# A later first branch hint and a finer last output block in a convolution and token-mixing kernel

## The chip, the cores and the metric

The kernel runs on one core of a Trainium2 chip. The metric is device time in microseconds (us) of one execution. It is some 1.9 us longer than the span that the profile shows. "Faster" or "slower" means by over 2%.

## The reference

The input x has 8 batches of 4224 tokens with 192 channels. A causal convolution of 7 taps, one softmaxed set of taps for each of 8 heads of 24 channels, is followed by a linear attention without softmax, a ReLU and an output product.

```python
def _attn_ref(x, weight):                    # weight: (8 heads, 7 taps)
    ...                                      # w = softmax(weight) over the taps
    out = np.einsum('hk,bskhg->bshg', w, x_unf)        # causal, 6 zeros ahead
    ...
def _moe_ref(x, w_q, w_k, w_out):
    wq = x @ w_q;  wk = x @ w_k
    W_tok = scale * np.einsum('bsd,btd->bst', wq, wk)
    mixed = np.einsum('bst,btd->bsd', W_tok, x)
    return np.maximum(mixed, 0.0) @ w_out
```

As nothing stands between the two products of the attention, the kernel forms the small matrix of each batch (a Gram matrix of the convolved y, with w_q and w_k around it) and multiplies the tokens by that.

## The kernel before

One program of some 5700 instructions is laid out ahead of time by a planner in the kernel's file. The names that the profile shows: xw is a staged piece of x, "ps<-xw,band" the convolution as a matmul with a band matrix, "ps<-y" the Gram matmuls, "ps<-yb,wq" the query product (Q), "ps<-qt,m_sb" the mixing (Z), "ps<-wo,zt" the output product (O), o_sb an output slot. Eight output slots of 768 KB serve in turn.

Two places are changed. The first is the class that puts branches and their hints into TensorE's stream, which it counts in blocks of 256 instructions: the page has 2456 matmuls, as many weight loads, and 19 instruction packets of 16 KB. A branch that goes to the next instruction anyway carries a hint, which is meant to have the next block fetched ahead; in the execution that the prediction read the first hint ran at 0.91 us and the first 16 KB fetch started at 2.01. Before, the first hint is TensorE's first action:

```python
class Ahead:
    HEAD, BLOCK, FROM = 64, 256, 128
    def __init__(self, nc, e):
        ...
        e.reg_mov(self.reg, 0)
        self.mark = e.mark_branch_hint_location()      # at 0.9 us
    def step(self, waits):
        if self.n >= self.cuts * self.BLOCK + self.FROM:
            self.cut()                                 # the branch, and the next hint
        ...
```

The second is the last full output block, which is cut into two jobs of two PSUM banks with one store each:

```python
            for j in range(2):
                cols = slice(2 * q + j, 512, 4)
                ...
            elif tail:
                parts = [(at + 2 * q * D, [[4 * D, 128], [HALF * D, 2], [1, 2 * D]],
                          OUT[:, orr, q, :].rearrange("p (h d) -> p h d", h=2))]
```

GpSimd issues nearly all loads of x, and between them it clears some tiles, in this order:

```python
    load(1, 3)
    load(2, 0)
    z_wo2 = pool(lambda e: e.memset(WO2[:, :], 0.0))
    load(2, 1)
```

WO2 is a zero-padded copy of a part of the output weights. The copies into it wait for this memset, and the planner's ORDER string puts the evictions of the first mixing matrix (m_sb) behind those copies.

## Time and profile before

| | before |
|---|---|
| time, first three timed runs | 154.13 to 154.24 us, median 154.21 |
| time, 46 further runs over five chips | 154.10 to 156.47 us |
| execution that the prediction read | 155.59 us, span 153.7 |
| a usual execution, profiled later | 154.22 us, span 152.3 |

The kernel has two kinds of execution: most take 154.1 to 155.0 us, and 14 of the 49 that were timed in all took 155.6 to 156.5. The page that the prediction read came from one of the second kind, while the time that it started from is of the first. The record lists the mean granted clock of nearly every run: it is 0.973 to 0.978 in all 19 long runs of the kernels that clear WO2 on GpSimd, and 0.984 or more in 70 of their 72 others. A stretch at half clock like the one on that page (0.50 from 11.75 to 15.16 us) takes 0.011 off the mean of a span of 153.7; so my estimate from these figures is that a long execution has one in it (and two usual ones too). Of the profiled executions that have one, those of r3 and r4 below are listed with 0.976 (155.92 us, long) and 0.975 (154.33 us, usual), that of the page with 0.982. In the prediction's lines a number pair such as "9.28 0.02" is a start and a duration in us, and in the windows there follow each engine's busy time and its instructions, the clock, the share of the DMA engines and GB/s.

### The profile page before, as it was taken

Reading aid. Unit: us, or ns where it says so; the run is one execution under the profiler, and the core shown is the slowest. Engines: PE = TensorE matmul, PEld = TensorE weight load, DVE = VectorE, ACT = ScalarE, POOL = GpSimd, SP = SyncE. Lnnn points to the kernel's source line nnn. Section 1 sums busy time; section 2 is a strip of 40 time slices with the busy share of each in tenths; the row PEclk is TensorE's granted clock in tenths of the full one; section 3 lists DMA queues with packets and bytes.
Section 4 is the critical chain, followed back from the end, with each engine's and each line's share of the span. In section 5 each row is a group of like instructions: output and inputs, shape, how many; then the busy total and the mean of one; then the engine's idle time right before and its main releaser. Section 6 shows DMA issues by size and latency. Waiting matters only on the chain.

```text
span 153.7 us, 5694 instructions
## 1 busy us (share of the span) xinstructions
PE 139.9 (91%) x2456; PEld 101.9 (66%) x2456; DVE 119.8 (78%) x239; ACT 128.2 (83%) x213; POOL 58.4 (38%) x76
## 2 busy tenths in 40 slices
PE   5647897999999999999999999999999999999930
PEld 1337774877777777677777777668677778775720
DVE  6544898988998878798989877999998988695800
ACT  5443869999998989989998989899899788999950
POOL 7999999997367620817200021120020200000000
PEclk9995999999999999999999999999999999999997
DMA  3999999999999999999999999999999967499795
GB/s 96 263 196 181 190 190 183 190 191 193 191 193 191 238 341 340 266 189 279 340 341 221 206 343 340 295 175 363 404 389 408 334 241 291 174 390 396 289 376 212
DMA packets 48440, 40.83 MB, mean 266 GB/s; under 512 B 37280, under 2 KB 40480, under 8 KB 48416
## 3 DMA queue, kind: packets, MB, share of 16 engines
q0 software_dynamic: 36384, 13.35, 73.4%
q1 hardware_dynamic: 12032, 27.14, 48.5%
q8 instruction: 19, 0.31, 0.7%
q14 instruction: 5, 0.04, 0.1%
HBM read 27.86 MB, written 25.95 MB: 350 GB/s over the span
## 4 chain that ended last, share of the span: by engine, by line
PE 78%; DVE 7%; DMA 5%; ACT 3%; issue 1%; SPq 1%; ACTq 0%
PE ps L194 78%; DMA o_sb<-in_x_dram 5%; DVE y L1021 2%; ACT y L1021 2%; DVE yb L1017 1%; DVE zt L1025 1%; DVE zr L1025 1%; DVE m_sb L1027 1%; DVE o_sb L1021 1%; ACT o_sb L1021 1%; DVE qt L1021 1%; DVE xw L1021 0%; ACT m_sb L1026 0%; ACTq L154 0%; ACT wo L1021 0%
## 5 line engine op out<-in xcount | busy, mean ns | idle before, releaser
L1021 ACT COPY o_sb<-ps 128x768 f32<-128x768 f32 (+1 forms) x61 | 47.3, 788 | 3.7 <-PE ps L194 2.6
L194 PE MATMUL ps<-wo,zt 128*128 128x192 bf16 (+1 forms) x358 | 47.5, 270 | 0.3 <-DVE o_sb L1021 0.2
L194 PEld LDWEIGHTS ps<-y 128*128 128x128 bf16 (+1 forms) x864 | 36.3, 99 | 12.5 <-issue 2.5
L1021 ACT CAST y<-ps 128x864 bf16<-128x864 f32 (+6 forms) x47 | 38.0, 834 | 7.5 <-PE ps L194 7.0
L194 PE MATMUL ps<-y 128*128 128x64 bf16 (+1 forms) x864 | 40.9, 195 | 1.2 <-DVE y L1021 1.2
L194 PEld LDWEIGHTS ps<-wo,zt 128*128 128x128 bf16 x358 | 31.9, 114 | 9.3 <-ACT zt L1024 0.7
L1017 DVE STREAM_TRANSPOSE yb<-y 128x576 int32<-128x576 int32 x48 | 35.7, 759 | 0.1
L194 PE MATMUL ps<-xw,band 128*128 128x432 bf16 (+5 forms) x192 | 32.3, 290 | 3.6 <-DVE xw L1021 2.0
L1021 POOL COPY y<-y 128x1152 bf16<-128x1152 bf16 x11 | 12.6, 1146 | 59.8 <-ACT y L1021 40.0
L1025 DVE TENSOR_SCALAR zt<-ps 128x512 bf16<-128x512 f32 x44 | 29.3, 679 | 4.8 <-PE ps L194 4.5
L326 POOL DMA_DIRECT2D xw<-in_x_dram x35 | 32.1, 928 | 2.0 <-POOL xw L485 1.1
L1024 ACT ACTIVATE zt<-ps 128x512 bf16<-128x512 f32 x52 | 30.3, 604 | 1.5 <-PE ps L194 1.4
L194 PE MATMUL ps<-qt,m_sb 128*128 128x512 bf16 (+2 forms) x120 | 30.8, 344 | 0.5 <-ACT m_sb L1026 0.5
L1021 DVE CAST y<-ps 128x864 bf16<-128x864 f32 (+2 forms) x21 | 21.5, 1024 | 3.6 <-PE ps L194 3.1
L194 PEld LDWEIGHTS ps<-xw,band 128*128 128x128 bf16 x192 | 13.8, 100 | 8.8 <-DVE xw L1021 2.3
L1021 DVE CAST qt<-ps 128x288 bf16<-128x288 f32 (+1 forms) x32 | 12.3, 425 | 7.2 <-PE ps L194 7.2
L194 PE MATMUL ps<-yb,wq 32*64 32x288 bf16 x768 | 15.2, 284 | 0.3 <-ACT y L1021 0.3
L1021 ACT CAST qt<-ps 128x576 bf16<-128x576 f32 x16 | 10.3, 643 | 3.4 <-PE ps L194 2.7
L194 PEld LDWEIGHTS ps<-qt,m_sb 128*128 128x128 bf16 (+1 forms) x120 | 8.9, 96 | 5.0 <-ACT m_sb L1026 0.8
L194 PEld LDWEIGHTS ps<-yb,wq 32*64 32x64 bf16 x768 | 10.5, 102 | 2.6 <-issue 0.7
L194 PE MATMUL ps<-warm 128*128 128x256 bf16 (+1 forms) x21 | 6.4, 420 | 1.3 <-DVE warm L377 1.3
L1021 DVE COPY o_sb<-ps 128x192 f32<-128x192 f32 (+1 forms) x11 | 6.8, 618 | 0.9 <-PE ps L194 0.6
(65 smaller groups left out, 72.8 us busy)
## 6 DMA issues: line engine op xcount, KB each, us to landing
out_dram<-o_sb SPq DMA_DIRECT2D x31, 768.0 KB, 7.2
xw<-in_x_dram POOLq DMA_DIRECT2D x14, 432.0 KB, 15.9
xw<-in_x_dram POOLq DMA_DIRECT2D x14, 384.0 KB, 16.9
o_sb<-in_x_dram SPq DMA_DIRECT2D x2, 480.0 KB, 6.0
out_dram<-o_sb SPq DMA_DIRECT2D x16, 48.0 KB, 5.7
out_dram<-o_sb SPq DMA_DIRECT2D x2, 384.0 KB, 3.0
xw<-in_x_dram POOLq DMA_DIRECT2D x2, 240.0 KB, 8.3
xw<-in_x_dram POOLq DMA_DIRECT2D x1, 288.0 KB, 6.9
```

Source lines behind the costliest of these rows:

```text
L194: return self.e.matmul(*a, **k)
L326: return e.dma_start(XW[lo:hi, b % NX, half, c : c + n, :], bass.AP(x_t, at, [[D, hi - lo], [CW * D, n], [1, D]]),)
L1017: return e.transpose(o, i)
L1021: return e.copy(o, i) if eng == "act" else e.tensor_copy(o, i)
L1024: return e.activation(o, i, AF.Relu)
L1025: return e.tensor_scalar(o, i, 0.0, None, op0=ALU.max)
L1027: else e.tensor_scalar(o, i, scale, None, op0=ALU.mult))
```

## The change

It has two intents: to keep the 16 KB instruction fetch (1155 ns from 2.01 us in the execution that the prediction read) away from the first loads of x, by having the hint behind the first band matmuls, and to shorten the end, by four one-bank jobs whose evictions start sooner. The planner's constants are fitted anew.

```diff
-    HEAD, BLOCK, FROM = 64, 256, 128
+    HEAD, BLOCK, FIRST, HINT, FROM = 64, 256, 0, 106, 132
...
-        self.mark = e.mark_branch_hint_location()
+        self.mark = None
...
     def matmul(self, *a, **k):
+        if self.inside:
+            at = self.n - self.cuts * self.BLOCK
+            if self.mark is None and at >= self.HINT:
+                self.hint()
+            if at >= (self.FROM if self.cuts > self.FIRST else self.HINT + 26):
+                self.cut()
...
-            for j in range(2):
-                cols = slice(2 * q + j, 512, 4)
+            for j in range(1 if tail else 2):
+                cols = slice(q if tail else 2 * q + j, 512, 4)
...
-                parts = [(at + 2 * q * D, [[4 * D, 128], [HALF * D, 2], [1, 2 * D]],
-                          OUT[:, orr, q, :].rearrange("p (h d) -> p h d", h=2))]
+                parts = [(at + q * D, [[4 * D, 128], [HALF * D, 2], [1, D]],
+                          OUT[:, orr, q // 2, 384 * (q % 2) : 384 * (q % 2) + 384]
+                          .rearrange("p (h d) -> p h d", h=2))]
...
-    "dma": (377e3, 13.2, 1.6, {"x": 2.2, "o": 1.2}), "fetch": (64, 256, 5.5, 3.5, 120.0),
+    "dma": (377e3, 13.2, 1.6, {"x": 2.2, "o": 1.2}), 
+    "fetch": (64, 256, ((26.0, 8.5), (98.0, 6.4), (121.0, 7.3), (999.0, 4.8))),
```

More of the change, by code (lines that the diff above doesn't have):

```diff
@@ L25 @@
     "DYGGGYGGGTMAMYOOZZZGGGZDQOTZGOGAOGZTGTGAGGGQGZEOZOMZOZMOZOTZZZOOZOZOQZOZZZOOZZZO"
-    "ZOOOO"
+    "ZOOOOOO"
 )
 CLOCK = {
-    "x0": (5.0, 7.5, 9.0, 8.1, 10.2, 12.0, 13.1, 13.8), "band": 6.5, "wq": 14.0, "wk": 16.0,
-    "wo": 20.5, "fill": 24.0,
-    "dma": (377e3, 13.2, 1.6, {"x": 2.2, "o": 1.2}), "fetch": (64, 256, 5.5, 3.5, 120.0),
+    "x0": (5.0, 7.5, 8.9, 8.1, 10.0, 11.8, 12.8, 13.6), "band": 6.5, "wq": 14.0, "wk": 16.0,
+    "wo": 22.5, "fill": 24.0,
+    "dma": (377e3, 13.2, 1.6, {"x": 2.2, "o": 1.2}),
+    "fetch": (64, 256, ((26.0, 8.5), (98.0, 6.4), (121.0, 7.3), (999.0, 4.8))),
 }
@@ L163, in _emit @@
         for o in self.ops[name]:
-            if ahead:
-                ahead.step(len(waits[o]))
             for sem, val in waits[o]:
                 e.wait_ge(sem, val)
+            if ahead:
+                ahead.op(len(waits[o]))
             last = o.fn(ahead or e)
@@ L186, in __init__, with op @@
         self.n = self.HEAD + 1
-        self.cuts = 0
-        self.reg = e.alloc_register("trip")
-        e.reg_mov(self.reg, 0)
-        self.mark = e.mark_branch_hint_location()
-    def matmul(self, *a, **k):
+        self.cuts = self.FIRST
+        self.never = e.alloc_register("never")
+        e.reg_mov(self.never, 0)
+        self.mark = None
+        self.inside = False
+    def op(self, waits):
+        self.n += max(0, waits - 1)
+        self.inside = False
+    def matmul(self, *a, **k):
+        if self.inside:
[4 more added lines that the diff above has]
+                self.cut()
+        self.inside = True
         self.n += 2
@@ L197, in to, with hint @@
         self.nc.switch_bb(name, parent=self.parent)
-    def step(self, waits):
-        if self.n >= self.cuts * self.BLOCK + self.FROM:
-            self.cut()
-        self.n += max(0, waits - 1)
+    def hint(self):
+        self.n += 1
+        self.mark = self.e.mark_branch_hint_location()
     def cut(self):
@@ L206, in cut @@
         self.cuts += 1
-        self.n += 2
-        self.e.br_eq(self.reg, 2, f"code_{j + 2}", f"code_{j}").branch_hint(self.mark)
+        self.n += 1
+        self.e.br_eq(self.never, 1, f"code_{j + 2}", f"code_{j}").branch_hint(self.mark)
         self.to(f"code_{j}")
-        self.mark = self.e.mark_branch_hint_location()
+        self.hint()
     def close(self):
@@ L675, in job_q @@
         return Job(
-            ("Q", b, g), 4, pe, [288] * 6,
+            ("Q", b, g), 4, pe, [292] * 6,
             reads=["wq"] + [("TD", b, 3 * g + k) for k in range(3)],
@@ L796, in job_o @@
         rem = i == 4
+        tail = b == B - 1 and i == 3
         def pe(e, bk):
@@ L819, in make @@
             if tail:
-                return [(
-                    OUT[:, orr, q, :].rearrange("p (h r d) -> p r h d", h=2, r=2),
-                    PS[:, bk : bk + 2, 0:384].rearrange("p r (h d) -> p r h d", h=2),
-                )]
+                return [(OUT[:, orr, q // 2, 384 * (q % 2) : 384 * (q % 2) + 384], PS[:, bk, 0:384])]
             return [(
@@ L827, in make @@
             )]
-        tail = b == B - 1 and i == 3
         def then():
@@ L858, in then @@
             queue["o"].append((max(o.end for o in evs) + DELAY,
-                               (64 * 2 * D if rem else 128 * 4 * D if tail else 128 * 8 * D) * 4,
+                               (64 * 2 * D if rem else 128 * 2 * D if tail else 128 * 8 * D) * 4,
                                landed, GATES.get(n, -1)))
@@ L863, in job_o @@
         return Job(
-            ("O", b, i, q), 1 if rem else 2,
-            pe, [192, 192] if rem else [192, 192, 384] * 2,
+            ("O", b, i, q), 1 if rem or tail else 2,
+            pe, [192, 192] if rem else [192, 192, 384] * (1 if tail else 2),
             reads=[("WO", k) for k in range(2)] + [("Z", b, i, k) for k in range(1 if rem else 3)],
-            evacs=[(make, ("OUT", b, i, q), 192 if rem else 768, "copy")],
+            evacs=[(make, ("OUT", b, i, q), 192 if rem else 384 if tail else 768, "copy")],
             then=then,
@@ L893, in bass_lightweight_conv__then__hypermixer_token_mlp_kernel @@
         "MC": [j for b in range(B) for j in (job_tr(b), job_mm(b))],
-        "O": [job_o(b, i, q) for b in range(B) for i in order(b) for q in range(2 if i < 4 else 1)],
+        "O": [job_o(b, i, q) for b in range(B) for i in order(b) for q in range(1 if i == 4 else 4 if b == B - 1 and i == 3 else 2)],
         "Z": [job_z(b, i, k) for b in range(B) for i in order(b) for k in range(3 if i < 4 else 1)],
@@ L949, in f @@
         def f(t):
-            x_at[id(xg[b][part])] = t - (b == 1) * (1.0 - 0.8 * (part == 2))
+            x_at[id(xg[b][part])] = t - (b == 1) * (0.3 - 0.1 * (part == 2))
             return x_at[id(xg[b][part])]
@@ L1027, in emit @@
                 else e.tensor_scalar(o, i, scale, None, op0=ALU.mult))
-    FIRST, BLOCK, AWAY, NEAR, CALM = CLOCK["fetch"]
+    FIRST, BLOCK, AWAY = CLOCK["fetch"]
     code = [FIRST + 2 * (16 + 1 + 20), 0.0, 0.0]
@@ L1040, in stall @@
             when = max(ok, when)
-            got = [when, when + (AWAY if when < CALM else NEAR)]
+            got = [when, when + next(v for u, v in AWAY if when < u)]
             edge += BLOCK
@@ L1194, in fused @@
         for fn, need, m, us, words in (
-            (tails, deps, "R", 0.2183 + 0.17 * n, 4 + 8 * n), (heads, late, "F", 0.33 * n, 8 * n),
+            (tails, deps, "R", 0.2183 + 0.17 * n, 4 + 8 * n), (heads, late, "F", 0.33 * n + 0.02, 8 * n),
         ):
```

## The prediction

Statements of the hardware that nothing in this case shows are cut from the recorded texts, and the cuts are marked: here a list of general statements that its observations were compared with, and the first rival's reason why TensorE might stand at instruction 512; in r5's text a cause of long executions. The sum: -1.9 us in the head, +0.5 in the middle and +0.1 in the tail make -1.3, so 152.9 us, taken as 152.8 for the half clock. In "it is hidden for TensorE", "it" is the fetch, and PE's timeline marks no wait from 18.26 to 22.37 us, with instruction 512 at 20.05.

> **What bounds the kernel now.** I read the page first (engine shares, slices, queues), then the chain of waits in order of time, then the timeline and the windows of the two ends, and last the trace's records of DMA packets and of landings one by one.
>
> ```profile
> PE 139.9 (91%) x2456; PEld 101.9 (66%) x2456; DVE 119.8 (78%) x239; ACT 128.2 (83%) x213; POOL 58.4 (38%) x76
> PE   5647897999999999999999999999999999999930
> PEclk9995999999999999999999999999999999999997
> DMA  3999999999999999999999999999999967499795
> q8 instruction: 19, 0.31, 0.7%
> out_dram<-o_sb SPq DMA_DIRECT2D x2, 384.0 KB, 3.0
> ```
>
> TensorE is busy 91% of the span; a slice is 3.8 us, so all the room is in the first seven slices and the last two. The DMA row is at 9 from the second slice to the 32nd: the transfers are saturated until about 120 us and a second bound lies close behind TensorE. The 19 instruction packets are 16 KB each.
>
> The chain of waits starts so:
>
> ```profile
> 1.66 7.62 DMA o_sb<-in_x_dram
> 9.28 0.02 issue
> 9.30 0.74 DVE xw L1021
> 10.04 0.04 issue
> 10.09 0.61 PE ps L194 x8
> 10.70 0.02 issue
> 10.72 1.55 DVE y L1021 x3
> 12.27 0.05 issue
> 12.32 2.59 PE ps L194 x38
> ...
> 24.99 81.44 PE ps L194 x1430
> ```
>
> The reader is to see that the second staged load of x holds the head until 9.28 us, that VectorE's cast waits only for it, and that from 24.99 us TensorE alone is the chain. The landing records of that load show 15 of its 16 increments between 6.36 and 6.87 us and the last at 9.28. The first load has 15 by 4.83 and the last at 5.56. The loads after it have one straggler too (7.50 and 9.57, 9.68 and 11.74, 12.61 and 14.38, 13.42 and 15.15). One of 16 DMA engines is about 2 us behind the others, and the packet list says why: the first 16 KB instruction fetch starts at 2.01 us and takes 1155 ns, while a 768-byte packet of x takes 36. That is 1155 / 36 = 32 of its packets, and from 4.5 us the straggler shares its engine with the other load queue (49 ns against 51, in turn), so the delay stretches to 9.28 - 6.87 = 2.41 us. The fetch follows TensorE's first branch hint, which the trace has at 0.91 us.
>
> The end, by windows (us; then each engine's busy time and instructions, clock, DMA share, GB/s) and timeline:
>
> ```profile
> 133.30:147.40 14.10, 13.80 (x159) 9.71 (x155) 10.06 (x23) 13.16 (x21) 0.00 (x0) 1.00 0.90 340
> 147.40:153.70 6.30, 0.00 (x0) 0.00 (x0) 0.00 (x0) 0.84 (x2) 0.00 (x0) 0.84 0.75 272
> 145.89 1.48 PE L194 MATMUL ps<-wo,zt 128*128 128x192 bf16 x12
> 146.74 1.50 ACT L1021 COPY o_sb<-ps 128x768 f32<-128x768 f32 x2 [0.24 <-PE ps L194]
> ```
>
> Both last evictions sit on ScalarE while VectorE is free, and they end at 148.24 us. But the two stores behind them are issued only at 148.90 and 149.53, because SyncE is held by the issue before (147.51 to 148.86), and the last packet ends at 152.39. From 133.3 us the packets fill 90% and more of the engines. So the last stretch is the draining of stores, not the eviction.
>
> [...] The trace has 16 KB packets and no gap of TensorE at a block's edge, so it is hidden for TensorE, but not for the load beside it. [...] The trace has half clock from 11.75 to 15.16 us, just behind the idle stretch that the late load makes.
>
> **The change, part by part.**
>
> *The first hint moves* from 0.91 us to behind the first band matmuls and one filler, about 7 us. Removed: 1155 ns from one engine while the two staged loads and the next ones run. Added: the same fetch later. Other hints wait 5 to 8 us for their fetch once the DMA is full (10.25 to 17.00, 18.45 to 23.09), so I put it at 9 to 14 us. The head step by step: x part 0 lands at 4.84 instead of 5.56, so ScalarE's cast (0.99) and band copy (0.40) end near 6.25, VectorE's band copies at 6.31, and the first band matmuls start at 6.3 instead of 6.93. Part 1 lands at 6.87 instead of 9.28; cast 0.73 plus starts gives matmuls at 7.7 instead of 10.09, and with the same 2.23 us to the first Gram matmuls these start at 9.9 instead of 12.32: 2.4 us sooner. They may then run at full clock (30 at 27 ns instead of 53, 0.8 us more). The loads bring the limit. Parts 5, 6 and 7 need 11.6, 12.6 and 13.4 us even without a straggler. Batch 1 comes next: its second part lands last at 20.50 (15 at 19.58) and is used at 21.83, its last at 25.41 and is used at 26.84, and the output weights land at 21.09 and their wait is at 22.41. These slacks are 1.3 to 1.4 us, plus what the straggler loses when it has one late fetch of 0.9 us in place of a deficit of 1.8 us: 1.3 to 2.2 us can be kept. I take 1.9 at 27 us.
>
> *The middle* keeps its order of matmuls and is TensorE's, so the shift travels. But the stores of 50 to 120 us run on saturated transfers, which do not come sooner because TensorE does. An output slot is used again after eight blocks. Of the evictions that wait for such a store the tightest is at 81.03 us, whose store lands at 80.29: 0.74 us. The next are 1.74 (99.23) and 1.90 (93.26). With 1.9 us of shift ScalarE stands 1.2 us at 80, less some 0.5 if the gates of the stores, which wait for the straggler too, open sooner. PSUM has other banks and TensorE doesn't feel all of it. I take off 0.5 us: 1.4 us reach the end.
>
> *The tail block* becomes four jobs of one bank. Matmuls: 12 before and 12 after, no difference. Evictions: two of 0.80 us in a row become four of about 0.45 us (384 instead of 768 columns, the fixed part kept; my estimate from those rows) that two engines share, so the last ends near 147.4 + 0.45 = 147.85 instead of 148.24. That 0.4 us is not on the path while SyncE and the transfers are behind. The stores: 512 packets of 1536 bytes at a mean of 68.2 ns, /16 = 2.18 us, become 1024 of 768 bytes at 36 to 40 ns, /16 = 2.3 to 2.6 us, so +0.1 to +0.4. A dip of the packets at 149.5 to 150.5 us (82 and 85% full) is worth 0.16 us and may be filled. Two more issues of about 0.55 us each keep about the pace of 0.6 us a store. Net 0 to +0.2 us; I take 0.1.
>
> *The planner's constants* (arrival times, fetch times) change which of ScalarE and VectorE takes an eviction, and nothing else: no instruction is added. I take 0, give or take 0.4 us.
>
> Sum: -1.4 + 0.1 = -1.3, thus 154.21 - 1.3 = 152.9 us. Rounded to 152.8, as the half clock may vanish as well.
>
> **The rivals.** *First: the late fetch simply hurts other loads or TensorE.* If the fetch comes by 9 us, parts 4 to 7 keep their stragglers and the head gains 1 us or less; [...] TensorE may stand at instruction 512 (reached at 20.05 us now). For it: the planner's fetch time for the head rises from 5.5 to 8.5 us. Against it: at 24.24 and 31.23 two hints stood open with one fetch missing, and both were served. It makes the time 153.5 to 155. *Second: the DMA is the true bound.* The saturated rows and the 0.74 us slack speak for it; PSUM's buffering and the dips in the DMA row at 120 to 134 us against. Then about 0.7 us is kept: 153.6. *Third: the whole head moves up*, as the Gram chain gains 2.4 us and full clock 0.8, and the stores' gates open sooner with the straggler gone: 151.2 to 151.6. The landings of batch 1 speak against more than 2.2 us.
>
> **Range and chances.** The centre is 152.8. The range from 151.4 (third rival, no loss at 80 us) to 154.1 (first rival, mild) holds these. Faster by over 2% means under 151.13 us, or 3.1 us of gain, more than any slack of batch 1 allows: 0.1. Slower by over 2% would need TensorE standing for 3 us in the fetch: 0.02. Within 2%: 0.88.
>
> **What would show it.** The second staged load should land near 6.9 us, VectorE's cast start near 6.9 and the second group of band matmuls near 7.7; half clock at 11.75 us should shorten or go. No 16 KB packet should stand before 8 us. The last batch-1 load should land at 24.5 us. ScalarE or VectorE should wait for an output store near 79 to 80 us. At the end, two evictions each on ScalarE and VectorE, and 768-byte packets that end less than 0.3 us sooner against TensorE's last matmul. The prediction is wrong if the straggler is there without an early fetch, if TensorE stands at the edge of a block before 25 us, or if the shift at 27 us reaches the end whole.

## The result, and the profile after

The changed kernel took 154.43 to 154.56 us (four runs) against 154.13 to 154.28 of the kernel before beside it (four runs). The ratio is 1.0019, with a 95% interval of 1.0001 to 1.0036. A ratio here is the mean time of one kernel's fast runs over that of the other's of the same rounds, so not quite the ratio of the medians that are quoted. Of the kernel before's long executions all but one (156.47) count as fast, so they stand in the ratios of the experiments. The expected gain of 1.4 us is not there, and in these runs 0.3 us are lost.

The page of the kernel after, its engine shares, slices, DMA row and last stores:

```profile
PE 139.1 (91%) x2457; PEld 100.8 (66%) x2457; DVE 119.6 (78%) x241; ACT 128.4 (84%) x212; POOL 59.5 (39%) x77
PE   5777788999999999999999999999999999999920
PEclk9999999999999999999999999999999999999995
DMA  3999999999999999999999999999999978499896
out_dram<-o_sb SPq DMA_DIRECT2D x4, 192.0 KB, 2.4
```

The half clock is gone from the fourth slice and nothing else on the page stands out; the DMA row is as full as before. Its chain of waits, in order of time (start, duration, what), from the head of the kernel:

```profile
18.00 0.91 POOL xw L338
...
19.63 1.99 POOL xw L338 x2
21.62 0.48 POOL wo L534
22.11 0.02 issue
22.13 0.80 DVE wo L1030
...
23.20 0.36 DVE m_sb L1036
23.56 0.05 issue
23.60 3.58 PE ps L207 x48
```

No load of x stands in this chain. GpSimd issues loads one after the other and reaches the memset of WO2 at 21.62 us, VectorE copies the weights into it and only then evicts m_sb, and the first Z matmul starts at 23.60.

The same stretch of the kernel before, in a usual execution, as the chain of the first experiment shows it:

```profile
19.64 1.99 POOL xw L326 x2
21.63 0.48 POOL wo L522
22.11 0.02 issue
22.14 0.35 ACT wo L1021
...
22.89 0.32 ACT m_sb L1026
...
23.68 6.35 PE ps L194 x80
```

It is the same chain to within 0.08 us. In the execution that the prediction read, the late load and the half clock had pushed TensorE's own work past this point (24.99 us), so GpSimd did not appear.

The end of the kernel after, by the same windows as in the prediction (which are of a slower execution, hence the other shares):

```profile
133.30:147.40 14.10, 12.47 (x143) 8.66 (x140) 9.49 (x21) 12.60 (x22) 0.00 (x0) 1.00 0.96 366
147.40:153.70 6.30, 0.00 (x0) 0.00 (x0) 0.00 (x0) 0.00 (x0) 0.00 (x0) 0.57 0.59 189
```

and its timeline there (the copies of 128x384 are a tail job's evictions; ScalarE's five are two of 768 and three of 384 columns):

```profile
143.56 2.99 ACT L1030 COPY o_sb<-ps 128x768 f32<-128x768 f32 x5
144.48 1.50 PE L207 MATMUL ps<-wo,zt 128*128 128x192 bf16 x12
145.36 0.56 DVE L1030 COPY o_sb<-ps 128x384 f32<-128x384 f32 x1 [0.46 <-PE ps L207]
```

The last eviction ends at 146.55 us against 146.87 in the usual execution of before, with the last matmul at 145.65 and 145.66. The evictions are sooner by 0.32 us, as wanted. Yet the span ends 6.98 us after the last matmul starts, against 6.65 before.

The milestones of the profiled executions in us, read from the traces' landings and first matmuls. "Part" counts the pieces of batch 0's x from zero; a part has landed when the last of its increments has come, 16 for each load, as many as there are DMA engines on the page (in the execution that the prediction read, 15 of part 1's had come by 6.87 us and the last at 9.28, and the cast started at 9.30); r1, r9, r10 and r13 are experiments below.

| | before, as predicted from | before, usual (r1) | after | r9 | r10 | r13 |
|---|---|---|---|---|---|---|
| first 16 KB fetch starts | 2.01 | 2.69 | 10.57 | 2.04 | 10.55 | 13.52 |
| part 1 of x landed | 9.28 | 7.89 | 7.24 | 7.39 | 7.26 | 7.01 |
| part 5 of x landed | 13.51 | 12.74 | 12.78 | 12.45 | 12.85 | 12.01 |
| first Q matmul | 19.41 | 17.63 | 17.62 | 16.82 | 17.62 | 16.20 |
| first Z matmul | 24.99 | 23.68 | 23.60 | 22.91 | 23.44 | 28.79 |
| first O matmul | 28.63 | 27.36 | 27.44 | 26.32 | 26.93 | 32.19 |
| last matmul | 147.03 | 145.66 | 145.65 | 144.79 | 145.46 | 150.72 |
| end of the span | 153.68 | 152.31 | 152.63 | 151.45 | 152.11 | 157.47 |

### The profile page after: what moved, and what is told of

Its sections match the earlier page's. It is cut to its first block, busy times and chain, and to the rows that moved or that the text cites. A ratio compares the mean times of both kernels' runs of the same rounds, so it can differ in the third digit from the quotient of the medians.

```text
span 152.6 us, 5700 instructions
## 1 busy us (share of the span) xinstructions
PE 139.1 (91%) x2457; PEld 100.8 (66%) x2457; DVE 119.6 (78%) x241; ACT 128.4 (84%) x212; POOL 59.5 (39%) x77
## 4 chain that ended last, share of the span: by engine, by line
PE 75%; POOL 13%; DVE 5%; issue 2%; ACT 0%; ACTq 0%; POOLq 0%
PE ps L207 75%; POOL xw L338 7%; POOL wk L410 1%; DVE m_sb L1036 1%; DVE zt L1034 1%; POOL xw L355 1%; DVE zr L1034 1%; POOL wo2s L410 1%; DVE wo L1030 1%; DVE yb L1026 1%; DVE o_sb L1030 1%; DVE qt L1030 1%; POOL m_sb L523 0%; POOL wo L410 0%; POOL wq L520 0%
## 5 line engine op out<-in xcount | busy, mean ns | idle before, releaser
L1030 ACT COPY o_sb<-ps 128x768 f32<-128x768 f32 (+2 forms) x62 | 46.9, 772 | 3.5 <-PE ps L207 2.3
L1030 ACT CAST y<-ps 128x864 bf16<-128x864 f32 (+6 forms) x50 | 40.5, 838 | 5.3 <-PE ps L207 4.9
L207 PEld LDWEIGHTS ps<-y 128*128 128x128 bf16 (+1 forms) x864 | 35.6, 98 | 12.3 <-issue 2.4
L207 PE MATMUL ps<-y 128*128 128x64 bf16 (+1 forms) x864 | 40.2, 193 | 1.2 <-DVE yb L1026 0.6
L1030 POOL COPY y<-y 128x1152 bf16<-128x1152 bf16 x12 | 13.8, 1148 | 57.5 <-ACT y L1030 34.5
L1034 DVE TENSOR_SCALAR zt<-ps 128x512 bf16<-128x512 f32 x46 | 30.7, 680 | 5.5 <-PE ps L207 5.2
L1033 ACT ACTIVATE zt<-ps 128x512 bf16<-128x512 f32 x50 | 29.2, 604 | 1.8 <-PE ps L207 1.6
L1030 DVE CAST y<-ps 128x864 bf16<-128x864 f32 (+2 forms) x18 | 18.4, 1023 | 4.5 <-PE ps L207 4.1
L207 PEld LDWEIGHTS ps<-xw,band 128*128 128x128 bf16 x192 | 13.2, 98 | 8.4 <-DMA xw<-in_x_dram 1.6
L1030 DVE COPY o_sb<-ps 128x192 f32<-128x192 f32 (+2 forms) x12 | 7.4, 613 | 1.3 <-PE ps L207 1.0
```

What stands on the lines that cost most here:

```text
L207: return self.e.matmul(*a, **k)
L1030: return e.copy(o, i) if eng == "act" else e.tensor_copy(o, i)
L1033: return e.activation(o, i, AF.Relu)
L1034: return e.tensor_scalar(o, i, 0.0, None, op0=ALU.max)
```

## The experiments

All eighteen kernels gave correct results. Runs of one chip share the runs of the kernel before. Each text stands first, then what came.

### The parts of the change, one by one

**r1: the kernel before again.**

> The kernel before, unchanged, submitted as if it were a change. Theory A (the profiled execution of before that I read, 155.59 us with a span of 153.7, was an unusual slow one, and its usual execution of 154.2 us has no late second staged load): most of its executions here have a time of 154.2 and a span near 152.4, and the second staged load lands near 7 us in their profile. Theory B (span and time differ by another amount in the two kernels, and the late load is in every execution of before): spans near 153.7 beside times of 154.2. Ratio to before 1.000 either way.

It took 154.16 to 154.70 us in five runs and 156.05 in one; the profiled run took 154.22. This is the usual execution in the table. Half clock ends at 6.21 us here and first Z is at 23.68: the 1.3 us between the two profiles of this one kernel are the very 1.4 us that the prediction wanted to gain.

**r2: the moved hint alone,** with the tail and the constants of before. The branches move a little too, as in the change.

```diff
-        self.mark = e.mark_branch_hint_location()
+        self.mark = None
...
+            if self.mark is None and at >= self.HINT:
+                self.hint()
```

> Before with the moved first hint alone (and cuts inside a group of matmuls). My prediction's mechanism as it stands in all executions: the second staged load lands near 7 us, time about 152.8 (ratio 0.991). Theory A: the head of the usual execution has nothing to gain, 154.0 to 154.4 (ratio 0.999 to 1.001), with the same early landing.

154.56 to 154.90 us, ratio 0.9988 (0.9943 to 1.0033): above both texts. First O at 27.43, against 27.36 in r1. The hint alone brings nothing in usual executions; its own profile loses 0.4 us at the end (7.03 us from the last matmul to the end of the span against 6.65), where the last instruction fetch took 1532 ns at 141.87 us and the last stores landed at 152.05 in one increment and by 151.64 in the others. That the fetch made this one late is my reading; whether it holds for the other five runs is not known.

**r3: the new tail alone.**

```diff
-            for j in range(2):
+            for j in range(1 if tail else 2):
...
-                parts = [(at + 2 * q * D, [[4 * D, 128], [HALF * D, 2], [1, 2 * D]],
+                parts = [(at + q * D, [[4 * D, 128], [HALF * D, 2], [1, D]],
```

> Before with the last output block in four one-bank jobs and four stores alone. My estimate: 0 to +0.2 us on the path, so 154.2 to 154.4 (ratio 1.000 to 1.0015). Rival: the earlier last eviction counts, -0.4 us (ratio 0.9975). Rival that blames the tail for the whole loss: +0.3 us or more (ratio 1.002).

Four runs at 154.50 to 154.74, two at 155.92 and 155.99. The four fit the rival that blames the tail for +0.3 us (five of r1's runs on this chip took 154.16 to 154.70). The profiled run is one of the slow ones: its half clock lies at 23.86 to 27.28 us, behind the wait for GpSimd, and first O is at 28.92. Its last matmul is 6.98 us ahead of the end of the span, as in the whole change.

**r4: the planner's constants alone.**

```diff
-    "wo": 20.5, "fill": 24.0,
+    "wo": 22.5, "fill": 24.0,
...
-            ("Q", b, g), 4, pe, [288] * 6,
+            ("Q", b, g), 4, pe, [292] * 6,
```

> Before with the planner's constants of the change alone (arrival, fetch and matmul times, which move evictions between ScalarE and VectorE). If these are neutral, 154.2 (ratio 0.999 to 1.001). If the loss is theirs, +0.3 us or more (ratio 1.002 or more).

Five runs at 154.18 to 154.45 and one at 156.26, ratio 0.9991 (0.9933 to 1.0049): nothing. Here half clock lies at 8.12 to 11.54 us and costs nothing at the end, since first Z is at 23.71 all the same (here ScalarE's casts of y end as late as GpSimd's chain does elsewhere).

**r5: the whole change again.**

> The change once more, beside before on one chip. My theory now: its head has no half clock where it counts, so no execution above 155.3, and the four small stores cost it 0.33 us: 154.4 to 154.7 in every execution, while before scatters from 154.2 to 156. Rival: the slow executions [...] come with the moved hint too, about one in four.

Five runs at 154.37 to 154.58, one at 155.88, ratio 1.0001 (0.9940 to 1.0062). The run of 155.88 is against the theory that no execution of the change is a long one.

**r6: hint and constants with the old tail.** The edit is the tail's part of the change, taken out.

> The change without its tail (last block in two jobs of two banks with two stores, as before). Theory: 0.33 us less than the change, 154.1 to 154.3, from the last matmul to the end 6.65 us instead of 6.98. Rival: the moved hint or its planner's constants cost by themselves, as the hint alone was at 154.6 to 154.9: then 154.5 or more.

154.27 to 154.49 us, a little above the text. The last matmul is 6.74 us ahead of the end.

**r7: four one-bank jobs, but two stores,** as before, of 1536-byte packets.

```diff
-                return [(OUT[:, orr, q // 2, 384 * (q % 2) : 384 * (q % 2) + 384], PS[:, bk, 0:384])]
+                return [(
+                    OUT[:, orr, q // 2, :].rearrange("p (h r d) -> p r h d", h=2, r=2)[:, q % 2],
+                    PS[:, bk, 0:384].rearrange("p (h d) -> p h d", h=2),
+                )]
...
-                parts = [(at + q * D, [[4 * D, 128], [HALF * D, 2], [1, D]],
+                parts = [(at + (q - 1) * D, [[4 * D, 128], [HALF * D, 2], [1, 2 * D]],
```

> The change with its four one-bank jobs but two stores of 1536-byte packets. Theory, the drain of packets is the end: as with the old tail, 154.1 to 154.3, although the last eviction ends 0.3 us sooner than there. Rival, the eviction is on the path: 153.8 to 153.9.

154.27 to 154.54 us, 6.74 us from the last matmul to the end, as r6. So the four evictions gain nothing, and in the profiles the four stores cost 0.24 us against r6 and r7 and 0.33 against r1. In the times the cost is smaller than the scatter can show: medians of 154.48 (r5), 154.41 (r6) and 154.32 (r7). The packets say how the stores cost: 1024 of 768 bytes at a mean of 38.9 to 39.5 ns, over 16 engines, are 2.49 to 2.53 us; 512 of 1536 bytes at 68.2 ns are 2.18. SyncE is not it: its four issues start at 147.56, 148.19, 148.71 and 149.25 us and the stores land at 150.02, 150.55, 151.13 and 151.68, so the last store goes into packets that already fill the engines (after's DMA share is 1.06 from 149.25 to 150.50 us, overlaps counted).

**r8: the kernel before, with the memset on VectorE.** This is the test of the chain that the page of after showed.

```diff
-    z_wo2 = pool(lambda e: e.memset(WO2[:, :], 0.0))
+    z_wo2 = dve(lambda e: e.memset(WO2[:, :], 0.0))
```

> Before with one change: the zeroing of the second output weights is done by VectorE in the head instead of by GpSimd behind its DMA issues (where it ends at 22.1 us in all profiles). Theory, this GpSimd chain holds the first use of M at 23.6 to 23.7 us whatever the loads do: the first matmul of Z moves to 22.8 to 22.9 us, the shift travels through the middle, 153.3 to 153.6 us in the fast executions. Rival, the middle takes the shift (output slots near 79 us with 0.5 us of slack): 153.9 to 154.2. Rival, the head is bound elsewhere: Z stays at 23.6 and the time at 154.2.

153.53 to 154.53 us, median 154.02 against 154.63, ratio 0.9960 (0.9904 to 1.0016). First Z comes at 23.04 instead of 23.68 and first O at 26.69 instead of 27.36; the median lies in the range of the first rival, though the profile shows no wait for an output slot. One word changed moved the head by 0.7 us with the hint where it was, while the hint's move brought nothing. The interval still reaches 1; r9 and r18 settle it.

### The moved hint once GpSimd is out of the way

Theory then: the hint gains as soon as the memset no longer hides it. Four kernels, all with the memset on VectorE, went to one chip with five rounds.

**r9: that kernel again, early hint** (the edit of r8).

> The kernel before with the zeroing of wo2 on VectorE and not on GpSimd, once more, as the early-hint side of a pair (its hint stays at 0.9 us). My theory: the head of the kernel before is set by GpSimd's chain that ends in this memset, and once it is gone the second load of batch 1 sets it, whose last increment scatters with the early 16 KB instruction fetch. So 153.5 to 154.5 us as in the earlier look, median near 154.0, with now and then a run above 155.3. Rival (the earlier gain was chance): median within 0.1 us of the kernel before's undisturbed runs, 154.2 or more.

153.25 to 154.75 us, median 153.71 against 154.51, ratio 0.9934 (0.9886 to 0.9983). The gain of r8 was no chance. Its chain of waits in the head:

```profile
11.13 8.49 DMA xw<-in_x_dram
19.62 0.05 issue
19.67 0.56 PE ps L194 x4
...
22.29 0.47 DVE qt L1021
22.76 0.15 issue
22.91 6.22 PE ps L194 x85
```

GpSimd's memset is gone from it; now the second load of batch 1, landed at 19.62 us, sets first Z.

**r10: the moved hint** (r2 and r8 together).

> The moved hint alone plus the zeroing on VectorE; planner's constants and tail of before. Theory that the moved hint helps only once GpSimd's chain is out of the way: against the same kernel with the early hint 0.2 to 0.6 us lower in the median and a narrower spread, no run above 155.3. Rival (the moved hint does nothing, or its other order of fetches costs as much as it brings): same median as the early-hint kernel of this call, within 0.15 us. If its last instruction fetch again falls at 142 us on one lane of the last store, 0.3 us of that are lost at the end, which the last landing increments would show.

153.73 to 154.37 us, median 154.00. The spread is narrower, as expected, but the median is 0.29 us higher than r9's, not lower: the theory fell. (Ratio to before 0.9949, 0.9905 to 0.9993.) Its chain:

```profile
5.26 7.59 DMA xw<-in_x_dram
12.85 0.05 issue
12.89 0.77 PE ps L206 x8
...
20.19 2.76 DVE y L1032 x3
22.95 0.38 DVE qt L1032
23.33 0.11 issue
23.44 6.32 PE ps L206 x85
```

Part 5 of batch 0, landed at 12.85 us (12.45 in r9), now heads the chain. The moved fetch starts at 10.55 us, while the packets of that part are under way: 30 of the part's 32 increments were in by 11.56, the other two came at 12.69 and 12.85. Parts 2 to 4 land sooner than in r9 (8.69, 7.88 and 9.82 against 9.25, 8.71 and 10.67), parts 5 to 7 later (12.85, 13.59 and 14.35 against 12.45, 13.33 and 14.09). Over all eight profiles with the hint at this place, part 5 landed at 12.76 to 12.86; with the early hint at 12.19 to 13.51.

Part 5 is not the whole of it. Among those eight profiles first Q came at 17.62 to 17.64 in four (after, r5, r10, r11) and at 16.96 to 17.19 in the others (r2, r6, r7, r12), with the same landings. What differs is a copy of y by VectorE, here in r10, with what GpSimd does then, and in r12:

```profile
16.39 0.82 DVE L1032 COPY y<-y 128x256 bf16<-128x256 bf16 x1
16.37 0.76 POOL L522 MEMSET m_sb<- 128x768 bf16 x1
...
16.28 0.18 DVE L1030 COPY y<-y 128x256 bf16<-128x256 bf16 x1
16.62 0.76 POOL L523 MEMSET m_sb<- 128x768 bf16 x1
```

In the four late profiles, as in r1 and r18, this copy starts after GpSimd's clearing of m_sb has begun, takes 0.59 to 0.83 us in place of 0.18, and ends some 0.1 us after the clearing does. So VectorE seems to wait for GpSimd there; no run moved that memset to test it. Where the copy came first, with the memset of WO2 on VectorE too (r12), first Z was at 22.80, no later than in r9.

**r11: hint, constants, old tail** (r6 and r8 together).

> Moved hint, the planner's constants, old tail, zeroing on VectorE. Theory: 153.4 to 153.7 us with a spread under 0.3 us, first Z matmul at 22.9 us or sooner in place of 23.6 to 23.8; it is then the fastest of all versions in the median. Rival (the second load of batch 1 lands when the DMA rate lets it, hint or no hint): 153.9 to 154.3 us, first Z at 23.0 to 23.3, and the chain of waits goes through that load.

153.77 to 154.60 us, median 153.91; part 5 at 12.79, first Z at 23.43. Ratio 0.9946 (0.9901 to 0.9990). Level with r10, so the expectation of 153.4 to 153.7 fell with the theory.

**r12: the whole change** (r5 and r8 together).

> The whole change plus the zeroing on VectorE: moved hint, constants, four one-bank jobs and four stores. Theory: as the version with the old tail in this call, plus the 0.3 us that the 768-byte packets of the four stores cost (last matmul to the end of the span 6.98 us in place of 6.65 to 6.74), so 153.7 to 154.0 us. Rival (the tail's cost is hidden or smaller when the head is earlier): no difference to the version with the old tail.

153.24 to 154.22 us, median 154.12 (ratio 0.9939, 0.9893 to 0.9985), that is 0.21 above r11 (7.17 us from the last matmul to the end against 6.72, in single profiles). This profile shows one thing more. Its head is among the earliest (first O at 26.42), and its chain of waits, asked for up to 82 us, runs so:

```profile
66.76 0.47 SPq L858
67.23 0.04 issue
67.28 12.34 DMA out_dram<-o_sb
79.62 0.02 issue
79.64 0.02 ACTq L166
79.65 0.04 issue
79.69 0.80 ACT o_sb L1030
```

ScalarE had waited 0.85 us for a store of 12.34 us to leave its output slot. The view of waits has the same wait with 0.7 us in r9 and 0.8 in r16, whose first O is at 26.3 us. It has none from 70 to 82 us in r1, r8, r10, r11, r18 and the kernel after, whose first O is at 26.69 or later. From the fourth batch's Q to the fifth's, TensorE took 20.4 us in r1, 20.6 in r9 and 21.0 in r12, so 0.2 to 0.6 us of an earlier head are given back there.

### Where the fetch goes

What was open then: does the fetch at 10.55 us delay part 5, or is that part late by itself?

**r13: the hint still later,** behind TensorE's instruction 200, memset on VectorE.

```diff
-    HEAD, BLOCK, FIRST, HINT, FROM = 64, 256, 0, 106, 132
+    HEAD, BLOCK, FIRST, HINT, FROM = 64, 256, 0, 200, 132
```

> Moved hint, moved further back (behind instruction 200 of TensorE in place of 106), zeroing on VectorE, planner's constants and tail of before. Theory A (the fetch at 10.6 us is what delays the fifth input load): the first 16 KB fetch falls at 13 us or later, the second half of the fifth load lands by 12.3 us in place of 12.85, first Q matmul at 16.8 us or sooner in place of 17.62, first Z at 22.5 to 22.9, and the time is 153.2 to 153.6 us with a narrow spread. Theory B (the fifth load is late by the transfers' own rate): it lands at 12.7 to 12.9 again and the time stays at 153.9 to 154.1. Both fall if TensorE stands at the edge of its third block (instruction 512, about 18 us) because the fetch comes too late; that would be a wait of TensorE there and 154.5 us or more.

159.21 to 161.00 us. Both halves of the text came true. Part 5 landed at 12.01 and first Q came at 16.20, the earliest of all (r17 has it too). Then, in PE's timeline:

```profile
16.20 0.93 PE L206 MATMUL ps<-yb,wq 32*64 32x288 bf16 x43
22.07 0.46 PE L206 MATMUL ps<-yb,wq 32*64 32x288 bf16 x5 [4.93 <-issue]
```

TensorE stands 4.93 us at its instruction 512, the edge of the third block (counted from the trace's records and the 64 instructions that the class takes to be ahead of them). The two first hints had run at 10.29 and 10.77 us and the fetches started at 13.52 and 19.66; the standing ends 1.5 us behind the second of them (20.55).

**r14: the same with the memset on GpSimd.**

> The same later hint with the memset still on GpSimd. Theory (GpSimd's chain sets the head, whatever the loads do): first Z matmul at 23.6 to 23.8 us again and 154.2 to 154.5 us, although the fifth load lands sooner. Rival (the loads set it): as the version with the zeroing on VectorE, under 153.8 us.

159.58 to 160.67 us; TensorE stood 4.59 us at the same place, so neither side of the text could be tested. Part 5 landed at 12.45. Part 1 landed at 8.15 us here, one increment 1.27 us behind the fifteenth, with no fetch before 13.5 us. An early fetch is then not the only cause of a late increment; the other is not known.

**r15: r13 with the constants.**

> The later hint, zeroing on VectorE and the change's planner constants, old tail. Theory: the constants only move evictions between ScalarE and VectorE, so within 0.2 us of the same kernel without them, 153.2 to 153.7 us if theory A of the later hint holds, 153.8 to 154.1 if theory B does.

158.86 to 160.46 us: the standing again, 5.52 us at the same place, so the constants could not be judged. Part 5 landed at 12.59.

**r16: hint behind instruction 150, first branch at 240.**

```diff
-    HEAD, BLOCK, FIRST, HINT, FROM = 64, 256, 0, 106, 132
+    HEAD, BLOCK, FIRST, HINT, FROM = 64, 256, 0, 150, 132
...
-            if at >= (self.FROM if self.cuts > self.FIRST else self.HINT + 26):
+            if at >= (self.FROM if self.cuts > self.FIRST else 240):
```

> Zeroing on VectorE, hint behind instruction 150 and the first branch (with the second hint behind it) at 240, so that some 2 us lie between the two hints. Theory C (TensorE stood because the second hint came 0.5 us behind the first and only one fetch was made ahead): no wait of TensorE at instruction 512, the first fetch at 12 to 14 us, the fifth load landed by 12.5 us, first Q by 16.9, and 153.2 to 153.7 us, that is level with or up to 0.4 us below r18. Theory D (a hint behind some 100 instructions is too late in any case): TensorE stands at 17 to 18 us for over 3 us and the time is above 157.

Two runs took 153.55 and 153.70 us, four 155.90 to 162.28. In the profiled run (153.55) the fetch starts at 12.77, part 5 lands at 11.56, nothing stands, and first Z is at 22.86: level with r9, not below it, as the second load of batch 1, landed at 19.56, sets it as in r9 (19.62). That load landed at 19.48 to 19.75 in 17 of the 20 profiles, wherever the hint was. The fetch now delays part 7 instead, landed at 14.81 against 13.27 in r17.

**r17: hint behind 200, branch at 246.**

> The same with the hint behind instruction 200 and the branch at 246. Between the two hints lies some 1 us. Theory C: as r16 if that is enough, a wait of TensorE at instruction 512 if it is not. Theory D: it stands as in r13, 159 us or more.

One run took 153.68, five 161.01 to 162.85, too few fast ones for a ratio. The profile is of a long one; PE's timeline has

```profile
25.23 0.44 PE L206 MATMUL ps<-xw,band 128*128 128x216 bf16 x3
30.72 0.36 PE L206 MATMUL ps<-xw,band 128*128 128x216 bf16 x1 [5.06 <-issue]
```

It passed instruction 512 without a wait and stood at 768, the next edge, with the fetch for it at 28.29. So neither theory holds as it was put: more room between two hints helps at one edge, and the later hints' fetches come behind in turn. What rule the fetcher follows with open hints stays open.

**r18: the early hint with the memset on VectorE,** beside them.

> The kernel before with the zeroing on VectorE and its early hint, as the one to compare with on the same chip: 153.3 to 154.6 us, median 153.7 to 154.0 as in two earlier calls, first Z at 22.9 to 23.1 us.

153.49 to 154.49 us, median 154.01 against 154.55, ratio 0.9931 (0.9879 to 0.9982). The profiled run (154.49) was at half clock until 11.01 us, had first Q at 18.36 and first Z at 24.18. The text had first Z at 22.9 to 23.1. This is the spread of that version: a head that GpSimd no longer pins there shows the clock and the loads (and here the copy of y took 0.75 us again).

The version of r8, r9 and r18 is the simplest of the fast ones: 18 runs, 153.25 to 154.75 us, median 153.90 and below before's in all three. With the moved hint (r10 to r12, 18 runs) it is 153.24 to 154.60, median 154.02, so the two are level. Part of the ratios is before's long executions: against its usual runs alone (up to 155.3 us) the medians of r8, r9 and r18 are lower by 0.25, 0.78 and 0.31 us. None of these 36 runs was above 155.3. With the memset on GpSimd 18 of 67 runs with the early hint were (before, r1, r3, r4) and 1 of 28 with the hint at 106 (after, r2, r5 to r7). So the moved hint makes long executions rarer, and the memset on VectorE does too: in the 36 runs the mean clock is 0.985 or more, so none had the stretch of half clock. Why the memset does it was not tested by itself, though r3's half clock lay just behind the wait that the memset makes.

## Why the prediction was wrong, point by point

**The starting point.** The 9.28 us of part 1 and the half clock at 11.75 us were real, but of a long execution; the time of 154.21 was of usual ones. A usual execution has part 1 at 7.89 and first O at 27.36. The gain that was predicted is what usual executions do not lose, and the page's own span of 153.7 said so.

**The head: this step failed.** The prediction put it as "The loads bring the limit" and "I take 1.9 at 27 us". At 27 us nothing was gained: first O 27.44 against 27.36. In place of the loads, GpSimd's chain of issues and the memset of WO2 set first Z at 23.6, hint or no hint (23.60 to 24.17 with the hint at 106). That was shown in two ways: the chain of both kernels runs through it, and r8, r9 and r18 undo it and gain 0.4 to 0.7% on three chips (two of the three intervals lie wholly below 1; a part of this is long executions that stay away). The prediction did see a wait for the output weights (at 22.41 us) but asked only when they landed, not what the copy behind them waited for.

**The early steps of the head** were right, also against usual executions: part 0 landed at 4.94 (predicted 4.84), and over all profiles at 4.83 to 4.94 with a later hint, at 5.35 to 6.26 with the early one. Part 1 landed at 7.24 (predicted 6.9; 6.80 to 8.17 over the eight profiles with the hint at 106), the second group of band matmuls started at 8.04 (predicted 7.7), no 16 KB packet came before 8 us, the fetch came at 10.57 (predicted 9 to 14), and the last batch-1 load landed at 24.49 (predicted 24.5). Half clock went. One of the prediction's own signs of being wrong came too, a straggler without an early fetch: part 1 at 8.17 in r2, 8.07 in r5 and 8.15 in r14.

**The first rival, that the late fetch hurts other loads or TensorE,** is right too, behind the first limit. r10 against r9 shows the load: part 5 0.4 us later, first Q 0.8 later, of which the rest is the copy of y. r13 shows TensorE at instruction 512, as that rival feared, but only with a later hint than the change has; with the fetch behind it (r13 to r17) part 5 landed at 11.56 to 12.59 us, so the fetch was what delayed it, by 0.2 to 1.3 us. So the moved hint had little to give in either place: with the memset on GpSimd, first Z is pinned by it; without it, a first Z of some 22.9 is set by batch 1's second load, hint or no hint (r9, r16, r17), and r10 and r11 came 0.5 us behind that, by part 5 and the copy of y together. How much of this is the hint's own is not shown.

**The middle.** The prediction took off 0.5 us for a slot at 80 us. In the change there was no shift to lose, and no wait for a store near 79 to 80 us. With an earlier head, ScalarE waited 0.85 us at 79 us (r12): mechanism, engine and place were right.

**The tail.** It was taken as +0.1 and came as +0.24 to +0.33 us in the profiles. The evictions ended 0.32 us sooner, near the predicted 0.39, and off the path, as said; but ScalarE had three of the four, not two (0.48 us each for 384 columns and 0.56 on VectorE, against 0.80 and 0.94 for 768; 0.45 was estimated). The mis-sized term is the one of the packets: 2.49 to 2.53 us is within the predicted 2.3 to 2.6, but the prediction took a low value and let a dip of 0.16 us be filled, which it was not.

**The constants,** 0 give or take 0.4: r4 agrees. **The sum** was then not -1.3 but about 0 from the head, 0 from the middle and +0.3 from the tail, and the measured medians differ by 0.27.

## What to carry to other kernels

Before reading a profile for its bound, compare its span with the timed runs: if it is a long execution, its waits are those of long executions, and what looks like a gain may be only the usual run. When a late arrival is to be removed, look for the next thing that the same instruction waits for, the memsets and issues of an engine that is off the path too; here undoing it took one word. A transfer that is moved away from one load landed on another here (part 5 at 12.85 us in r10 against 12.45 in r9, part 7 at 14.81 in r16 against 13.27 in r17), and stores at the very end were better few with large packets (2.18 us of packets for two stores against 2.49 to 2.53 for four).

## What the runs showed of the hardware

- With the first hint at 0.91 us TensorE did not wait at instruction 512 (before, 20.05 us). With hints behind its instruction 200 TensorE stood 4.93 us at instruction 512 (r13) and 5.06 us at 768 (r17); how far ahead instructions are held is not shown. The fetch is one packet of 16 KB, which took 879 to 1155 ns in the traces of before and after and 1532 ns at the end of r2, and a load's or a store's last increment came late beside it (part 0 at 4.83 to 4.94 us without an early fetch, 5.35 to 6.26 with one).
- The first fetch started 1.1 us (r9, hint at 0.91 us) to 4.3 us (r15, hint at 10.57 us) behind its hint, and with a hint that came late the same kernel took 153.6 us or up to 162.9 (r16 and r17).
- Half clock at 11.75 to 15.16 us (before, 155.59, with a late load as well) came with a time 0.9% above 154.2, and at 23.86 to 27.28 us (r3, 155.92) 0.8% above r3's usual 154.7. The place counted: half clock at 8.12 to 11.54 us cost nothing (r4, 154.33).
- Stores of 768 bytes took 38.9 to 39.5 ns a packet, 1536 bytes 68.2 ns: 19.4 to 19.7 bytes a ns against 22.5, so the smaller ones were some 13% slower.
